# Last rows of four batches in one output block, and the last modes copied by halves on two engines

## The chip, the cores and the metric

The kernel runs on one core of one Trainium2 chip. The metric is device time in microseconds (us) of one execution. Five engines work beside each other: TensorE (PE, with its weight loads shown as PEld), VectorE (DVE), ScalarE (ACT), GpSimd (POOL), and SyncE (SP), which here only issues transfers. Matmuls read SBUF and write PSUM, which has 8 banks of 128 x 512 numbers in float32; ACT and DVE bring results from there to SBUF; 16 DMA engines move data between SBUF and device memory (HBM).

## The reference

```
scores = q @ k^T / sqrt(64) + decay(f), causal          # 8 batches, 8 heads, 576 rows, 64 wide
x      = softmax(scores) @ v          -> (8, 576, 512)
X      = rfft(x, axis=1)[:, :64]                        # 64 modes
Yr, Yi = complex product of X with w_r, w_i             # one 512 x 512 matrix pair for each mode
y      = irfft(Y, n=576)
u      = x + y
out    = u + relu(u @ w_ch)
```

The weights w_r and w_i of the 64 modes are by far the largest input: 64 pairs of 512 x 512 float32 matrices.

## The kernel before

A first phase computes the attention for 32 pairs of heads, and already multiplies the modes with those weights that have come in. A second phase streams the rest of the weights. Modes are taken in 16 units of four. Twelve units (96 rows of real and imaginary parts, `KF`) are folded early, batch by batch, by the inverse transform into `x_all` (which holds x and then x plus these modes) and into `XW` (the same times w_ch). The last four units (32 rows, `KL`) are left for the end, since their weights come last.

The end is what the change touches. It runs over output blocks: `blocks` is a list of (p, sb), where p is a pair of batches and sb one of five row blocks of 128, 128, 128, 128 and 64 rows. Each block needs, for each of its two batches, a PSUM tile `U` (u) and a tile `Z` (u times w_ch):

- `bases(n)` (matmuls at L788) starts the sums with `x_all` and `XW` through an identity. The row block of 64 rows is handled for two batches in one tile: one in rows 0 to 63, one in rows 64 to 127.
- `rest(n, U, Z)` (L803) adds the last modes: a matmul of depth 32, with the inverse transform `BI4` and the mode tile `yl`. `yl[h][0]` is for U and `yl[h][1]` for Z, h being a half of the batches (0 to 3, 4 to 7); each tile holds four batches, 32 rows each.
- ACT copies U to `u_sb` (L857); DVE computes max(Z, 0) + u_sb into `o_sb` (L858); SP issues the output transfer (L863, 512 KB for both batches of a full block; L868, two transfers of 128 KB for a block of 64 rows).

`last_modes(h)` makes the two `yl` tiles. Four matmuls with the identity turn the modes `YL` into `pyl` (L815). Eight matmuls with w_ch give `pywl` (L826): for each of four steps over the depth, one matmul for rows 64 to 127 and one for rows 0 to 63. Then ACT copies `pyl` to `yl[h][0]` (L834), and DVE copies `pywl` to `yl[h][1]` (L835). It is called for h = 0 ahead of the first block and for h = 1 ahead of block 7, counted from 0; the batches of half 1 begin with block 10.

The order of instructions on each engine is the order in which the program writes them (the schedule is manual). `psU` and `psZ` have four PSUM banks each, in turns; `pyl` and `pywl` take one each. The framework puts in the waits, among them those between writers of the same tile.

Of the kernel before, what the change touches and what calls it, by code (L numbers as in the profile page):

```python
# [10 lines left out]
F32 = mybir.dt.float32  # L11
BF16 = mybir.dt.bfloat16
# [11 lines left out]
def kernel(  # L24
# [11 lines left out]
    nc = tc.nc  # L36
    B, H, S, Dh = q.shape
    NM = moe_w_r.shape[0]
    D = H * Dh
    assert S == 576 and Dh == 64 and D == 512 and H == 8, (B, H, S, Dh)  # L40
    assert NM == 64 and B == 8
    NSB = 5
    SBLK = [128, 128, 128, 128, 64]
    NEB = D // 128
# [24 lines left out]
    wch = const.tile([128, NEB, D], BF16, name="wch")  # L69
# [8 lines left out]
    BI4 = const.tile([128, S], BF16, name="BI4")  # L78
# [547 lines left out]
    with ExitStack() as bctx:  # L626
# [3 lines left out]
        ylpool = bctx.enter_context(tc.tile_pool(name="ylpool", bufs=4))  # L630
        YT = ypool.tile([128, NEB, B, KF], BF16, name="YT")
        YL = ypool.tile([128, NEB, B, KL], BF16, name="YL")
        XW = {}

        with ExitStack() as mctx:
# [83 lines left out]
            for u in range(NU):  # L719
# [3 lines left out]
                first = 2 if u < NX else 1  # L723
                for dc in range(first, NEB - 1 if last else NEB):
# [3 lines left out]
                    if u >= NF and dc < 3:  # L728
                        b = 2 * (u - NF) + dc - 1
# [19 lines left out]
                for eb in range(NEB):  # L749
                    nc.tensor.matmul(  # L750
                        yps[:, eb, :],
                        lhsT=Yb[:, eb * 128 : (eb + 1) * 128],
                        rhs=perm[:],
                        start=True,
                        stop=True,
# [10 lines left out]
        usb = bctx.enter_context(tc.tile_pool(name="usb", bufs=4))  # L766
        psU = bctx.enter_context(tc.tile_pool(name="psU", bufs=4, space=PSUM))
        psZ = bctx.enter_context(tc.tile_pool(name="psZ", bufs=4, space=PSUM))
        blocks = [(p, sb) for p in range(B // 2) for sb in range(NSB)]
        yl = {}  # L770

        def parts(n):

            p, sb = blocks[n]
            Ms = SBLK[sb]
            if sb < NSB - 1:
                return [(2 * p + k, k, slice(0, Ms), sb, Ms) for k in range(2)]
            return [(2 * p + k, 0, slice(Ms * k, Ms * k + Ms), sb, Ms) for k in range(2)]

        def bases(n):  # L780

            pts = parts(n)
            nt = 1 + pts[1][1]
            U = [psU.tile([128, D], F32, tag="u", name="U") for _ in range(nt)]
            Z = [psZ.tile([128, D], F32, tag="z", name="Z") for _ in range(nt)]
            for which, ps in enumerate((U, Z)):
                for b, k, rows, sb, Ms in pts:
                    nc.tensor.matmul(  # L788
                        ps[k][rows, :],
                        lhsT=ident_bf[:Ms, :Ms],  # L790
                        rhs=XW[b][:Ms, sb, :] if which else x_all[:Ms, :, b, sb, :],
                        start=True,
                        stop=False,
                    )
            return U, Z

        def rest(n, U, Z):

            for which, ps in enumerate((U, Z)):
                for b, k, rows, sb, Ms in parts(n):  # L800
                    r = (b + 2 * which) % 4
                    grp = slice(32 * r, 32 * r + 32)
                    nc.tensor.matmul(  # L803
                        ps[k][rows, :],
                        lhsT=BI4[grp, sb * 128 : sb * 128 + Ms],
                        rhs=yl[b // 4][which][grp, :],
                        start=False,
                        stop=True,
                    )

        def last_modes(h):

            py = psU.tile([128, D], F32, tag="u", name="pyl")
            for eb in range(NEB):
                nc.tensor.matmul(  # L815
                    py[:, eb * 128 : (eb + 1) * 128],
                    lhsT=YL[:, eb, 4 * h : 4 * h + 4, :].rearrange("p b c -> p (b c)"),
                    rhs=ident_bf[:, :],
                    start=True,
                    stop=True,  # L820
                )
            pyw = psZ.tile([128, D], F32, tag="z", name="pywl")
            for eb in range(NEB):
                for n in range(2):
                    b = 4 * h + 2 * (1 - n)
                    nc.tensor.matmul(  # L826
                        pyw[64 * n : 64 * n + 64, :],
                        lhsT=YL[:, eb, b : b + 2, :].rearrange("p b c -> p (b c)"),
                        rhs=wch[:, eb, :],
                        start=(eb == 0),  # L830
                        stop=(eb == NEB - 1),
                    )
            yl[h] = [ylpool.tile([128, D], BF16, tag="yl", name="yl") for _ in range(2)]
            nc.scalar.copy(yl[h][0][:], py[:])  # L834
            nc.vector.tensor_copy(yl[h][1][:], pyw[:])  # L835

        first = bases(0)
        AT = psU.tile([128, NEB, 8, B], F32, tag="u", name="AT2")
        spec_cols(AT, NEB - 1)
        for h in range(2):  # L840
# [4 lines left out]
                accT[:, :, bs, :],  # L845
                ALU.add,
            )
        last_modes(0)
        for i, (p, sb) in enumerate(blocks):
            if i == 7:  # L850
                last_modes(1)
            U, Z = first if i == 0 else bases(i)
            rest(i, U, Z)
            o_sb = wpool.tile([128, 2, D], F32, tag="w8", name="o_sb")
            for n in range(len(U)):
                u_sb = usb.tile([128, D], F32, tag="usb", name="u_sb")
                nc.scalar.copy(u_sb[:], U[n][:])  # L857
                nc.vector.scalar_tensor_tensor(  # L858
                    o_sb[:, n, :], Z[n][:], 0.0, u_sb[:], ALU.max, ALU.add
                )  # L860
            s0 = sb * 128
            if len(U) == 2:
                nc.sync.dma_start(  # L863
                    out[2 * p : 2 * p + 2, s0 : s0 + 128, :].rearrange("b p e -> p b e"), o_sb[:]
                )
            else:
                for b, k, rows, _, Ms in parts(i):
                    nc.sync.dma_start(out[b, s0 : s0 + Ms, :], o_sb[rows, 0, :])  # L868


# [28 lines left out]
```

## Time and profile before

Three runs took 442.95, 443.5 and 444.18 us; the median is 443.5. The profiled execution took 443.21 us, of which 441.4 is the span from its first to its last instruction.

| what | before |
|---|---|
| profiled execution, span | 443.21 us, 441.4 us |
| PE, DVE, ACT, POOL busy, share of the span | 79%, 62%, 50%, 26% |
| DMA, mean rate | 219 GB/s |
| output transfers | 16 of 512 KB, 8 of 128 KB |
| first and last output transfer issued | 410.1 us, 436.1 us |

Times inside the span are counted from its first instruction. A row of the timeline gives the start, the busy time, the engine, the line and operation, the result and its sources, the shapes, how many instructions it merges, and in brackets how long the engine was idle before it and for whom. In the chain of waits, which is followed back from the last instruction, each row is a start, a length and the work; "issue" is time in which the engine waited for nothing that the profile shows. DMA shares are means over the 16 engines.

### The profile page before, as it was taken

Reading aid. Unit: us, or ns where it says so; the run is one execution under the profiler, and the core shown is the slowest. Engines: PE = TensorE matmul, PEld = TensorE weight load, DVE = VectorE, ACT = ScalarE, POOL = GpSimd, SP = SyncE. Lnnn points to the kernel's source line nnn. Section 1 sums busy time; section 2 is a strip of 40 time slices with the busy share of each in tenths; the row PEclk is TensorE's granted clock in tenths of the full one; section 3 lists DMA queues with packets and bytes.
Section 4 is the critical chain, followed back from the end, with each engine's and each line's share of the span. In section 5 each row is a group of like instructions: output and inputs, shape, how many; then the busy total and the mean of one; then the engine's idle time right before and its main releaser. Section 6 shows DMA issues by size and latency. Waiting matters only on the chain.

```text
span 441.4 us, 10293 instructions
## 1 busy us (share of the span) xinstructions
PE 349.8 (79%) x4305; PEld 192.2 (44%) x4305; DVE 275.3 (62%) x657; ACT 222.8 (50%) x339; POOL 113.1 (26%) x170
## 2 busy tenths in 40 slices
PE   1699787898898898888994495698798688888992
PEld 0456555554555565555552242243343233334330
DVE  6688999978887778888882231223313256464894
ACT  4444765586777765756650022033222265554672
POOL 6443434334433333434213111111202221100000
PEclk9999999999999999999998598599969699899997
DMA  8999999999999999999999999999999999994697
GB/s 205 205 230 229 219 228 230 229 218 228 221 226 230 227 220 229 218 230 218 206 212 212 212 212 211 213 212 212 212 212 210 210 209 210 211 210 86 238 365 258
DMA packets 70207, 96.77 MB, mean 219 GB/s; under 512 B 3536, under 2 KB 45008, under 8 KB 70160
## 3 DMA queue, kind: packets, MB, share of 16 engines
q0 software_dynamic: 60480, 77.08, 99.6%
q1 hardware_dynamic: 9680, 19.03, 12.5%
q8 instruction: 34, 0.56, 0.5%
q14 instruction: 13, 0.11, 0.1%
HBM read 163.73 MB, written 9.44 MB: 392 GB/s over the span
## 4 chain that ended last, share of the span: by engine, by line
DMA 36%; PE 36%; DVE 18%; issue 3%; ACT 3%; POOL 1%; DVEq 0%; POOLq 0%; ACTq 0%
DMA w<-in_moe_w_i_dram 22%; DMA w<-in_moe_w_r_dram 13%; DVE qkT L360 4%; DVE x_all L495 4%; PE pav L480 4%; PE A L194 4%; DVE vT L384 4%; PE sps L435 3%; PE tv L382 3%; PE pd L524 3%; PE vp L393 3%; DMA qk<-in_k_dram 2%; PE U L788 2%; PE Z L788 2%; DVE vn L372 2%
## 5 line engine op out<-in xcount | busy, mean ns | idle before, releaser
L442 ACT ACTIVATE et<-sps 128x1024 bf16<-128x1024 f32 x96 | 96.0, 1050 | 17.7 <-PE sps L435 13.1
L480 PE MATMUL pav<-vs,et 128*128 128x65 bf16 (+1 forms) x896 | 52.5, 199 | 0.0
L747 DVE TENSOR_TENSOR Yb<-A,yx 128x512 bf16<-128x512 f32 x15 | 10.4, 691 | 65.7 <-PE A L194 65.7
L360 DVE COPY qkT<-tp 128x640 bf16<-128x640 bf16 x64 | 48.7, 763 | 3.3 <-PE tp L355 3.3
L480 PEld LDWEIGHTS <-et 128*128 128x128 bf16 (+1 forms) x896 | 37.5, 103 | 18.1 <-issue 14.9
L194 PE MATMUL A<-w,XP 128*16 128x512 bf16 (+1 forms) x240 | 22.2, 450 | 24.9 <-DMA w<-in_moe_w_i_dram 14.2
L435 PE MATMUL sps<-qkT 64*128 64x512 bf16 (+4 forms) x320 | 40.3, 315 | 1.1 <-DVE qkT L360 1.1
L663 PE MATMUL pxw<-wch,xT 128*128 128x512 bf16 (+1 forms) x160 | 41.1, 412 | 0.0
L355 PE MATMUL tp<-ident_bf,qk 128*64 128x128 bf16 x576 | 30.3, 237 | 10.3 <-DMA qk<-in_k_dram 10.3
L495 DVE TENSOR_TENSOR x_all<-pav,rcp 128x384 bf16<-128x384 f32 (+2 forms) x96 | 36.2, 377 | 3.3
L384 DVE COPY vT<-tv 128x576 bf16<-128x576 bf16 x32 | 24.2, 757 | 18.9 <-PE tv L382 18.9
L156 POOL DMA_DIRECT2D w<-in_moe_w_r_dram x27 | 20.5, 757 | 51.9 <-DMA w<-in_moe_w_r_dram 16.1
L670 ACT CAST XW<-pxw 128x512 bf16<-128x512 f32 (+1 forms) x15 | 8.8, 584 | 47.6 <-PE pxw L663 47.6
L156 POOL DMA_DIRECT2D w<-in_moe_w_i_dram x27 | 20.3, 752 | 47.3 <-DMA w<-in_moe_w_i_dram 34.6
L670 ACT CAST yx<-pxw 128x512 bf16<-128x512 f32 (+1 forms) x25 | 14.6, 584 | 34.2 <-PE pxw L663 34.2
L165 POOL DMA_DIRECT2D w<-in_moe_w_r_dram x16 | 11.9, 741 | 71.2 <-PE A L194 56.8
L165 POOL DMA_DIRECT2D w<-in_moe_w_i_dram x19 | 13.2, 697 | 58.6 <-PE A L194 40.3
L709 ACT CAST x_all<-pu 128x512 bf16<-128x512 f32 (+1 forms) x40 | 23.4, 584 | 8.0 <-PE pu L708 7.0
L515 ACT CAST XS<-pd 128x192 bf16<-128x192 f32 x16 | 16.7, 1041 | 18.6 <-PE pd L508 18.5
L355 PEld LDWEIGHTS <-qk 128*64 128x64 bf16 x576 | 19.6, 117 | 14.1 <-issue 8.8
L109 POOL DMA_DIRECT2D qk<-in_q_dram x32 | 19.4, 606 | 24.0 <-PE tp L355 8.4
L372 DVE TENSOR_TENSOR vn<-vt,wn 128x576 bf16<-128x576 f32 x32 | 23.8, 744 | 2.7 <-ACT wn L297 2.7
(134 smaller groups left out, 645.6 us busy)
## 6 DMA issues: line engine op xcount, KB each, us to landing
w<-in_moe_w_r_dram POOLq DMA_DIRECT2D x16, 1024.0 KB, 29.6
w<-in_moe_w_i_dram POOLq DMA_DIRECT2D x15, 1024.0 KB, 32.2
w<-in_moe_w_r_dram POOLq DMA_DIRECT2D x27, 512.0 KB, 14.8
w<-in_moe_w_i_dram POOLq DMA_DIRECT2D x27, 512.0 KB, 14.6
vt<-in_v_dram SPq DMA_DIRECT2D x32, 288.0 KB, 5.8
out_dram<-o_sb SPq DMA_DIRECT2D x16, 512.0 KB, 4.0
qk<-in_q_dram POOLq DMA_DIRECT2D x32, 144.0 KB, 13.6
qk<-in_k_dram POOLq DMA_DIRECT2D x32, 144.0 KB, 13.7
```

The costliest lines, as they stand in the source:

```text
L156: nc.gpsimd.dma_start(w8[:, t, :, :], src[4 * u : 4 * u + 4, dc * 128 : (dc + 1) * 128, :].rearrange("m p e -> p m e"),)
L165: nc.gpsimd.dma_start(w8[:, j : j + step, :, :].rearrange("p m r e -> p m (r e)"), src[m : m + step, 256:512, :].rearrange("m (p r) e -> p ...
L194: nc.tensor.matmul(A[32 * j : 32 * j + M, :], lhsT=lhsT, rhs=rhs, start=st_, stop=sp_)
L355: nc.tensor.transpose(tp[64 * hp : 64 * hp + 64, r - r0, :, :].rearrange("p n c -> p (n c)"), qk[:, hp, r * 64 : r * 64 + 64], ident_bf[:, :],
L360: nc.vector.tensor_copy(st[i]["T"][:].rearrange("p n (c r) -> p n c r", r=9)[:, :, :, r0:r1], tp[:, 0 : r1 - r0, :, :].rearrange("p r n c ...
L372: nc.vector.tensor_tensor(vn[:], st[i]["vt"][:], _strided(wn[:, widx(i), :], [[1, 9], [0, Dh]]), ALU.mult)
L384: nc.vector.tensor_copy(st[i]["vT"][:].rearrange("p (c r) -> p c r", r=9), tv[:].rearrange("p r c -> p c r"))
L435: nc.tensor.matmul(ps[:, hp, c : c + n], lhsT=KT[sl, jb * 128 : jb * 128 + 128], rhs=QT[sl, i0 : i0 + n], start=True, stop=True,)
L442: nc.scalar.activation(st[i]["et"][:, T, :, :], ps[:], ACT.Exp, scale=scale)
L480: nc.tensor.matmul(pav[:Ms, sb % 3, hp, :], lhsT=eblk(i, hp, jb, sb), rhs=rhs, start=(jb == 0), stop=(jb == sb),)
L495: nc.vector.tensor_tensor(x_all[:ns, g, b, lo:hi, :].rearrange("p s (h d) -> p s h d", h=2), pav[:ns, lo % 3 : lo % 3 + n, :, 0:Dh], _stri ...
L663: nc.tensor.matmul(pxw[:Ms, :], lhsT=xT[:, eb, sb * 128 : sb * 128 + Ms], rhs=wch[:, eb, :], start=(eb == 0), stop=(eb == NEB - 1),)
```

## The change

The list of blocks gets another order and other blocks of 64 rows. For each half of the batches come the full blocks of its two pairs, eight in all, and then one block with the last 64 rows of four batches in two tiles. There are 18 blocks instead of 20, and as many matmuls and output results as before.

`last_modes` is taken apart. `modes_u(h)` makes `yl[h][0]`; `modes_z(h, n)` computes one half of the rows of `pywl`, with four matmuls, and `modes_z_keep(h, n)` copies that half. All copies go through `both`, which gives the left 256 columns to ACT and the right 256 to DVE. For h = 0, `modes_u` and the half with batches 0 and 1 stand ahead of block 0; the matmuls of the other half stand between block 0's U and Z matmuls, and its copy after block 0. For h = 1, `modes_u` stands after block 3, one half of `pywl` after block 4, the other after block 5. The first block is written by two transfers of 256 KB, each after its own result.

```diff
-        blocks = [(p, sb) for p in range(B // 2) for sb in range(NSB)]
+        blocks = []
+        for h in range(2):
+            blocks += [(p, sb) for p in (2 * h, 2 * h + 1) for sb in range(NSB - 1)] + [(h, NSB - 1)]
...
-            return [(2 * p + k, 0, slice(Ms * k, Ms * k + Ms), sb, Ms) for k in range(2)]
+            return [
+                (4 * p + 2 * k + m, k, slice(Ms * m, Ms * m + Ms), sb, Ms)
+                for k in range(2)
+                for m in range(2)
+            ]
...
-        def rest(n, U, Z):
+        def rest(n, ps, which):
...
+        def both(dst, src):
+            nc.scalar.copy(dst[:, 0 : D // 2], src[:, 0 : D // 2])
+            nc.vector.tensor_copy(dst[:, D // 2 : D], src[:, D // 2 : D])
+
-        def last_modes(h):
+        def modes_u(h):
+            yl[h] = [ylpool.tile([128, D], BF16, tag="yl", name="yl") for _ in range(2)]
             py = psU.tile([128, D], F32, tag="u", name="pyl")
...
+            both(yl[h][0], py)
+        pywl = {}
+        def modes_z(h, n):
+            if n == 1:
+                pywl[h] = psZ.tile([128, D], F32, tag="z", name="pywl")
+            half = slice(64 * n, 64 * n + 64)
+            b = 4 * h + 2 * (1 - n)
             for eb in range(NEB):
-                for n in range(2):
...
+        def modes_z_keep(h, n):
+            half = slice(64 * n, 64 * n + 64)
+            both(yl[h][1][half, :], pywl[h][half, :])
...
-        last_modes(0)
+        modes_u(0)
+        modes_z(0, 1)
+        modes_z_keep(0, 1)
         for i, (p, sb) in enumerate(blocks):
-            if i == 7:
-                last_modes(1)
-            U, Z = first if i == 0 else bases(i)
-            rest(i, U, Z)
+            U, Z = UZ if i == 0 else bases(i)
+            rest(i, U, 0)
+            if i == 0:
+                modes_z(0, 0)
+            rest(i, Z, 1)
...
+                if i == 0:
+                    nc.sync.dma_start(out[n, 0:128, :], o_sb[:, n, :])
...
+            if i == 0:
+                modes_z_keep(0, 0)
+            elif i == 3:
+                modes_u(1)
+            elif i == 4:
+                modes_z(1, 1)
+                modes_z_keep(1, 1)
+            elif i == 5:
+                modes_z(1, 0)
+                modes_z_keep(1, 0)
```

More of the change, by code (lines that the diff above doesn't have):

```diff
@@ L777, in parts @@
                 return [(2 * p + k, k, slice(0, Ms), sb, Ms) for k in range(2)]
-            return [(2 * p + k, 0, slice(Ms * k, Ms * k + Ms), sb, Ms) for k in range(2)]
+            return [
[3 more added lines that the diff above has]
+            ]
         def bases(n):
             pts = parts(n)
-            nt = 1 + pts[1][1]
-            U = [psU.tile([128, D], F32, tag="u", name="U") for _ in range(nt)]
-            Z = [psZ.tile([128, D], F32, tag="z", name="Z") for _ in range(nt)]
+            U = [psU.tile([128, D], F32, tag="u", name="U") for _ in range(2)]
+            Z = [psZ.tile([128, D], F32, tag="z", name="Z") for _ in range(2)]
             for which, ps in enumerate((U, Z)):
@@ L795, in bases @@
             return U, Z
-        def rest(n, U, Z):
[L799 to L809, printed above, removed]
-        def last_modes(h):
+        def rest(n, ps, which):
+            for b, k, rows, sb, Ms in parts(n):
+                r = (b + 2 * which) % 4
+                grp = slice(32 * r, 32 * r + 32)
+                nc.tensor.matmul(
+                    ps[k][rows, :],
+                    lhsT=BI4[grp, sb * 128 : sb * 128 + Ms],
+                    rhs=yl[b // 4][which][grp, :],
+                    start=False,
+                    stop=True,
+                )
+        def both(dst, src):
[3 more added lines that the diff above has]
+            yl[h] = [ylpool.tile([128, D], BF16, tag="yl", name="yl") for _ in range(2)]
             py = psU.tile([128, D], F32, tag="u", name="pyl")
@@ L821, in last_modes @@
                 )
-            pyw = psZ.tile([128, D], F32, tag="z", name="pywl")
-            for eb in range(NEB):
-                for n in range(2):
[L825 to L837, printed above, removed]
+            both(yl[h][0], py)
[5 more added lines that the diff above has]
+            b = 4 * h + 2 * (1 - n)
+            for eb in range(NEB):
+                nc.tensor.matmul(
+                    pywl[h][half, :],
+                    lhsT=YL[:, eb, b : b + 2, :].rearrange("p b c -> p (b c)"),
+                    rhs=wch[:, eb, :],
+                    start=(eb == 0),
+                    stop=(eb == NEB - 1),
+                )
+        def modes_z_keep(h, n):
+            half = slice(64 * n, 64 * n + 64)
+            both(yl[h][1][half, :], pywl[h][half, :])
+        UZ = bases(0)
         AT = psU.tile([128, NEB, 8, B], F32, tag="u", name="AT2")
@@ L847 @@
             )
-        last_modes(0)
+        modes_u(0)
+        modes_z(0, 1)
+        modes_z_keep(0, 1)
         for i, (p, sb) in enumerate(blocks):
-            if i == 7:
-                last_modes(1)
-            U, Z = first if i == 0 else bases(i)
-            rest(i, U, Z)
+            U, Z = UZ if i == 0 else bases(i)
[3 more added lines that the diff above has]
+            rest(i, Z, 1)
             o_sb = wpool.tile([128, 2, D], F32, tag="w8", name="o_sb")
-            for n in range(len(U)):
+            for n in range(2):
                 u_sb = usb.tile([128, D], F32, tag="usb", name="u_sb")
@@ L860 @@
                 )
+                if i == 0:
+                    nc.sync.dma_start(out[n, 0:128, :], o_sb[:, n, :])
             s0 = sb * 128
-            if len(U) == 2:
+            if sb == NSB - 1:
+                for b, k, rows, _, Ms in parts(i):
+                    nc.sync.dma_start(out[b, s0 : s0 + Ms, :], o_sb[rows, k, :])
+            elif i > 0:
                 nc.sync.dma_start(
@@ L865 @@
                 )
-            else:
-                for b, k, rows, _, Ms in parts(i):
-                    nc.sync.dma_start(out[b, s0 : s0 + Ms, :], o_sb[rows, 0, :])
+            if i == 0:
[8 more added lines that the diff above has]
+                modes_z_keep(1, 0)
 _INS = ['q', 'k', 'v', 'f', 'moe_w_r', 'moe_w_i', 'moe_w_ch']
```

## The prediction

> **What bounds the kernel now.** I read the page first. TensorE is busy 79% of the span and the weight stream keeps the DMA engines at about nine tenths to the 36th of 40 slices, so the body is set by loads that the change does not touch; the built programs are the same instruction for instruction up to the first `bases`. All the difference has to arise after the last weight has been used, at 404 us. Next I split what follows into stages, with each engine's busy time.
>
> ```profile
> 404.00:408.27 4.27, 3.21 (x48) 1.85 (x49) 1.27 (x4) 1.07 (x3) 0.00 (x0) 1.00 0.02 4
> 408.27:420.00 11.73, 11.73 (x80) 3.87 (x80) 9.54 (x16) 8.01 (x16) 0.00 (x0) 1.00 0.71 247
> 420.00:432.50 12.50, 12.50 (x86) 4.10 (x84) 11.66 (x20) 9.66 (x19) 0.00 (x0) 1.00 0.99 350
> 432.50:441.40 8.90, 0.77 (x8) 0.19 (x5) 2.40 (x4) 1.47 (x3) 0.00 (x0) 0.74 0.69 249
> ```
>
> The columns are the stage, its length, busy us (instructions) of PE, weight loads, DVE, ACT and POOL, then granted clock, DMA share and GB/s. From 408.27 TensorE has no free moment, and from 420 the DMA engines have none either (0.99): the stage has two limits, and the output queue is the later one. The vector engine ends at 434.91 (its last nine results start at 429.04 and take 5.87), but the last output transfer is issued at 436.1 and lands at 440.0. Then I read the chain of waits where the stage opens, and the timeline beside it.
>
> ```profile
> 406.05 0.41 PE pyl L815 x4
> 406.46 0.02 issue
> 406.48 0.59 ACT yl L834
> 407.08 0.45 issue
> 407.53 0.70 DVE yl L835
> 408.23 0.04 issue
> 408.27 0.39 PE Z L803 x2
> ```
>
> ```profile
> 406.38 1.05 PE L826 MATMUL pywl<-wch,YL 128*64 128x512 bf16 x8
> ...
> 408.74 1.29 DVE L858 SCALAR_TENSOR_TENSOR o_sb<-Z,u_sb 128x512 f32<-128x512 f32 x2 [0.52 <-PE Z L803]
> ...
> 410.06 4.92 SPq L863 DMA_DIRECT2D out_dram<-o_sb  x4
> ...
> 415.21 2.09 SPq L868 DMA_DIRECT2D out_dram<-o_sb  x2
> ```
>
> The first Z needs the vector copy of all of `pywl`, and the first transfer needs two vector results: nothing is written before 410.06. A full block then comes every 1.30 us (1.39 for one in four, where the Z matmuls show 0.69 us instead of 0.59). Last, the DMA view from 408 to 428 us, in 40 slices of 0.5 us:
>
> ```profile
> GB/s 0 0 0 0 0 25 373 377 275 147 348 336 361 389 365 389 389 373 258 74 229 303 385 410 401 393 258 307 381 369 385 381 336 250 295 397 389 402 410 356
> ```
>
> At 370 to 390 GB/s a 512 KB block takes 1.4 us, a little more than the engines need to make one. The queue thus falls behind by itself, unless a block is late: it ran nearly dry at 412.5, at 417.5 (74 GB/s) and, last, at 421 (258), where block 7 came late behind the second `last_modes`.
>
> **The change part by part.** The number of instructions of each kind is the same on TensorE; ACT and DVE have seven more each, all copies.
>
> *First modes, U.* One 0.59 us copy on ACT becomes two of 256 columns. DVE copies 128x256 from PSUM to bf16 in 0.42 (L761); for ACT no row has it, between 0.29 (half of 0.585) and 0.585: I take 0.35. In the built program the DVE half waits for the ACT half of the same tile, so 0.35 + 0.05 + 0.42 = 0.82, ending at 407.30. TensorE comes to the U matmuls only at 407.36, after `pywl`: cost nothing, with 0.06 us to spare. No row shows two engines reading one PSUM bank. [...]
>
> *First modes, Z.* Before, eight matmuls of 64 output columns alternate between the two halves of the array and take 0.98 us in the chain. A half alone is four. Their price lies between 0.49 (half of eight) and 1.03 (the four of L687, 96 columns wide, 0.88 in the chain). Of the 0.98 some 0.10 is the change from another kind of matmul, so a pair took 0.22, and that is what one matmul of 512 columns takes in the chain (L713, L705); I take 0.88 for four: the pairing was the saving, and it is lost. The first half thus ends where all eight did, 407.4. Copies 0.82: 408.25 (before 408.22). Now the new wait: in the built program the other half's matmuls wait for the DVE half of the first copy, since they write the same tile, and the block's Z matmuls are queued behind them on TensorE. 0.05 + 0.88 + 0.10 for the change of matmul kind (what L788 loses after L803): Z starts at 409.2 instead of 408.27, **+0.95**. DVE waits for Z, SP for DVE.
>
> *Block 0 in two transfers.* The first 256 KB goes out at 409.65 + 0.69 = 410.35, the second at 410.95. That is 0.3 later than before for the first, and there is nothing to gain from it unless block 1 follows sooner. It doesn't: its last Z takes over the bank of the first result (410.33 instead of 409.44), then 0.22 for that matmul, 0.10, 0.39 for U, 0.59 for `u_sb`, 1.29 for two results and 0.15 of hand-overs: 413.05 against 411.89, **+1.15**.
>
> *Second modes in three parts.* Before: one piece, 1.31 us of TensorE (416.13 to 417.44), and block 7 came 2.61 us after block 6 instead of 1.30. After: the U part 0.33, with its two copies in front of a U tile some 0.5; a Z part 0.88 + 0.10; a second one 0.98 plus 0 to 0.3 for the wait on the DVE half of the first, taken as 0.15. Sum 2.6, **+1.3**. TensorE has no idle time that could hide it. If a Z part were only 0.49 it would be 1.8, +0.5.
>
> *Last rows.* Four small blocks each took 0.89 of TensorE, 0.91 of DVE (0.61 and 0.30 idle). Two of four batches take 4 + 2 matmul slots, two results, some 1.45 each and 0.2 after the first: 3.1 against 3.6, **-0.5**. But runs of eight full blocks meet the 1.39 every second time: 3 or 4 more times 0.1, **+0.4**. The output transfers stay eight of 128 KB.
>
> Engines: 1.15 + 1.3 - 0.5 + 0.4 = +2.35, the last vector result at about 437.3.
>
> **From there to the end.** The queue counts, so I look for its last dry moment. Blocks after: 1 at 413.05, 2 at 414.35, 3 at 415.75, 4 at 417.55, 5 at 419.8, 6 at 422.25. Packets begin 0.92 after an issue (410.98 for 410.06), 1.4 per block: the queue is dry for 0.4 before block 4, 0.85 before 5, 1.05 before 6, and never again. Before, the same point was block 7, issued at 420.70. So 1.55 later. Left to write from there: before ten blocks and three pairs of 128 KB, 6.03 MB, in 421.6 to 440.0, or 328 GB/s with all its losses; after, ten blocks and eight of 128 KB, 6.29 MB, 0.8 us more. **+2.35** again. Against the profiled execution (443.21, of which 441.4 is span) that is 445.56; that execution lies 0.3 below the median of 443.5, and on the median I get 445.85, told as 445.9.
>
> **Bounds.** With the cheap ends (Z parts 0.49, copies side by side) block 6 comes about 1.5 us sooner; that leaves +1.0. If the queue's own unevenness before (about 1.6 us: the output packets' durations summed over 16 engines are 26.65 us, and with 410.98 and some 0.8 us of dry moments that ends at 438.4, not 440.0) is partly filled after, up to 1 us less: +0.4 to +1.3. On the other side SP took 1.12 to 2.16 us for a pair of small transfers; four in a row, some 3.6 us, may hold back block 9 by 1.2 and the end by 0.5: +4.
>
> **The rivals.** *The queue absorbs it.* The vector engine ended 5.1 us before the last landing, so 2.35 us later engines might hide behind the queue. For it: the share 0.99. Against it: what is dry early is not caught up, as the queue never has spare speed later. It holds if the queue is backed up at blocks 5 and 6; then only the later start and half of the rest are left, +0.6: 444.1. Chance 0.18.
>
> *Faster: the queue never runs dry.* If the three parts at blocks 4 to 6 fit into pauses that the modelled ends of matmuls hide, each hand-over stays under 1.4 us and the old dry moments at 417.5 and 421 vanish. From the first packet at 411, 9.44 MB at 385 GB/s are 24.5 us, two groups of small transfers 0.9 each, 0.35 to land: 437.7 against 440.0, -2.3, 441.2. It decides at the interval from block 3 to block 6: over 4.5 us it fails; I work out 6.5. For it speaks that a busy PE is modelled; against it PE 11.73 of 11.73. Chance 0.08.
>
> *The small transfers stall SP* (price above): +4, 447.5. For it: 2.16 for the last pair; against it: 1.12 for the second. Chance 0.10.
>
> **How the numbers follow.** The forecast, +1.3 to +3, has 0.64. The range leaves out a tenth on each side: from 444.1, the absorbed case, to 447.6, the stalled one. A measurement of this kernel tells 0.3%, 1.33 us, from no change. Slower by more: the forecast and the stall, 0.74. Within: the absorbed case, 0.18. Faster: 0.08.
>
> **What would show it.** Right: first Z at 409.2, four matmuls of a half in 0.88 and DVE's half behind ACT's; first transfers at 410.35 and 410.95, the next at 413.05; blocks 3 to 6 spread over 6.5 us with GB/s falling between them; last vector result at 437.3. Wrong: a half in 0.5 us, the first Z before 408.3, blocks 4 to 6 at an even 1.3 to 1.4 us, or GB/s above 350 from 412 to the end.

## The result, and the profile after

The changed kernel takes 446.74 us (median of 5, 446.46 to 446.89) against 443.96 (median of 5, 442.95 to 444.46): 2.8 us slower, a ratio of 1.0063 with a 95% interval of 1.0048 to 1.0077. Its profiled execution took 446.74 us, with a span of 445.0.

In that execution the first addition into `YL`, with which the tail opens, starts at 406.30 instead of 405.70. Up to there the two programs are the same, and that start varies between 405.7 and 408.3 over the executions below, so from here on positions are given **from the first YL addition** wherever two kernels are compared. The stages of the tail, cut 0.59 us later than in the prediction:

```profile
404.59:408.86 4.27, 3.22 (x44) 1.96 (x45) 1.36 (x5) 1.10 (x3) 0.00 (x0) 1.00 0.00 0
408.86:420.59 11.73, 11.23 (x62) 3.78 (x61) 8.90 (x17) 7.46 (x16) 0.00 (x0) 1.00 0.59 215
420.59:433.09 12.50, 12.50 (x81) 3.88 (x80) 10.90 (x18) 9.55 (x18) 0.00 (x0) 1.00 0.87 295
433.09:445.00 11.91, 3.35 (x29) 1.11 (x28) 4.82 (x8) 3.34 (x7) 0.00 (x0) 0.79 0.81 277
```

The columns are those of the prediction's table. In the second stage TensorE is again busy nearly throughout (11.23 of 11.73), but in the same time there are 62 matmuls where there were 80, and the output rate is 215 GB/s instead of 247; in the third it is 295 instead of 350. At full granted clock (1.00 in both stages), TensorE does something that takes longer. The chain of waits shows what:

```profile
406.65 0.40 PE pyl L825 x4
407.04 0.99 PE pywl L843 x4
408.04 0.03 ACTq L817
408.07 0.04 issue
408.11 0.38 ACT yl L817
408.48 0.02 issue
408.51 0.44 DVE yl L818
408.94 0.04 issue
408.99 1.04 PE pywl L843 x4
```

Four matmuls take 0.99 us where eight took 0.98. The kernel before has this row for its second modes, where TensorE comes to them without a wait:

```profile
416.46 0.98 PE pywl L826 x8
```

Matmul by matmul, the two of a pair start within 0.004 us of each other in the kernel before, and the next pair follows after 0.215 to 0.24. In the changed kernel each single matmul of a half takes a slot of that length for itself: the four start 0.240, 0.216 and 0.216 us apart.

ACT's copy and DVE's copy follow each other, and TensorE waits for the second of them before it starts the other half. Only after that comes Z, in the timeline:

```profile
409.94 0.39 PE L807 MATMUL Z<-yl,BI 32*128 32x512 bf16 x2
...
410.43 1.29 DVE L880 SCALAR_TENSOR_TENSOR o_sb<-Z,u_sb 128x512 f32<-128x512 f32 x2 [1.49 <-ACT yl L817]
410.71 0.84 PE L793 MATMUL Z<-XW,ident_bf 128*128 128x512 bf16 x2
411.15 0.94 SPq L884 DMA_DIRECT2D out_dram<-o_sb  x2
...
413.84 10.92 SPq L890 DMA_DIRECT2D out_dram<-o_sb  x7
```

The bracket names ACT's copy as the one that ended DVE's wait, but the result starts 0.49 us after the Z matmuls, much as before (408.74 after 408.27); it waits for Z, and the copy happened to end at the same moment. The Z matmuls of block 1 take 0.84 instead of 0.59: their second one waits for the bank of block 0's first result (it starts at 411.17, after the 411.12 at which that result ends), as foreseen. And the output rate from 408.6 to 428.6 us, 40 slices of 0.5 us:

```profile
GB/s 0 0 0 0 0 0 82 381 369 217 0 0 270 360 319 369 373 303 86 385 385 389 377 385 180 102 389 389 221 25 41 377 393 373 381 385 307 217 197 213
```

There are four holes instead of the old three: after block 0 (0 GB/s at 413.6 to 414.6), ahead of block 3 (86), of block 5 (102) and of block 6 (25 and 41). Those ahead of blocks 5 and 6 are where the prediction put them. The one that it put ahead of block 4 comes a block sooner: up to the slice with 86, 1.04 MB have passed since the first hole, which is blocks 1 and 2, and block 3's issue takes 0.99 us (416.53 to 417.52) where most take 0.37. The last three slices, 217 to 197, are something else; they come back at the end of this document.

| us from the first YL addition | before | after | later by | predicted |
|---|---|---|---|---|
| first Z matmuls start | 2.57 | 3.64 | 1.07 | 0.95 |
| second result of block 1 | 6.19 | 7.51 | 1.32 | 1.15 |
| last vector result | 29.21 | 31.87 | 2.66 | 2.35 |
| last landing | 34.32 | 37.39 | 3.07 | 2.35 |

### The profile page after: what moved, and what is told of

It reads as the page before. It is cut to its first block, busy times and chain, and to the rows that moved or that the text cites. A ratio compares the mean times of both kernels' runs of the same rounds, so it can differ in the third digit from the quotient of the medians.

```text
span 445.0 us, 10306 instructions
## 1 busy us (share of the span) xinstructions
PE 352.4 (79%) x4305; PEld 193.0 (43%) x4305; DVE 277.1 (62%) x661; ACT 224.3 (50%) x343; POOL 113.1 (25%) x170
## 4 chain that ended last, share of the span: by engine, by line
PE 37%; DMA 36%; DVE 18%; ACT 3%; issue 3%; POOL 1%; DVEq 0%; ACTq 0%; POOLq 0%
DMA w<-in_moe_w_i_dram 22%; DMA w<-in_moe_w_r_dram 13%; DVE qkT L360 4%; PE pav L480 4%; DVE x_all L495 4%; PE A L194 4%; DVE vT L384 4%; PE sps L435 3%; PE tv L382 3%; PE pd L524 3%; PE vp L393 3%; DMA qk<-in_k_dram 2%; PE Z L793 2%; PE U L793 2%; DVE vn L372 2%
## 5 line engine op out<-in xcount | busy, mean ns | idle before, releaser
L663 PE MATMUL pxw<-wch,xT 128*128 128x512 bf16 (+1 forms) x160 | 40.1, 405 | 0.0
L880 DVE SCALAR_TENSOR_TENSOR o_sb<-Z,u_sb 128x512 f32<-128x512 f32 x36 | 23.1, 686 | 4.7 <-ACT u_sb L879 2.5
```

Of the source, the lines that this page charges most:

```text
L663: nc.tensor.matmul(pxw[:Ms, :], lhsT=xT[:, eb, sb * 128 : sb * 128 + Ms], rhs=wch[:, eb, :], start=(eb == 0), stop=(eb == NEB - 1),)
```

## The experiments

All were run in five rounds beside the kernel before, whose median was 443.86 beside the first four, and 444.32 or 444.00 beside the others. The theory: TensorE's time counts in the tail, a half of the Z modes costs as much as the whole, and what is lost passes on to the end of the output. The first rival: the output queue (dry moments, small transfers in fours). The second: the copies in two serial halves. The third: the wait of Z behind the second half.

**Copies whole again.** From the changed kernel:

```diff
-            both(yl[h][0], py)
+            nc.scalar.copy(yl[h][0][:], py[:])
-            both(yl[h][1][half, :], pywl[h][half, :])
+            nc.vector.tensor_copy(yl[h][1][half, :], pywl[h][half, :])
```

> Changed kernel with the copies whole again: the U modes by ACT alone, each half of the Z modes by DVE alone over 512 columns. Theory (the loss is the matmuls of a half without a partner, 0.88 us each, and Z queued behind the second): a copy of 0.69 in place of 0.37 + 0.43 in a row, so the first Z comes some 0.1 to 0.15 us sooner, and the end 0.3 us sooner than in the changed kernel: +2.5 us against before. Rival (the copies by halves are the loss, since DVE waits for ACT each time): most of the 2.8 us goes, +0.5 us against before.

Measured: 446.95, ratio 1.0072 (1.0055 to 1.0090), no better than the changed kernel. The first Z comes 0.12 us sooner, as expected, but the 0.3 at the end does not appear: the last vector result stands at 31.96. In the second modes DVE's copy of 0.69 takes more of DVE's own time than a half of 0.43, which may be why; no run separates it. The copies by halves gain nothing, and they are not the loss.

**First modes as before.**

```diff
-        modes_u(0)
-        modes_z(0, 1)
-        modes_z_keep(0, 1)
+        modes_whole(0)        # eight paired matmuls, whole copies
...
-            if i == 0:
-                modes_z(0, 0)
...
-                modes_z_keep(0, 0)
```

> Changed kernel with the modes of the first four batches made as before (eight paired matmuls, whole copies, all ahead of block 0); the second modes stay in three parts. Theory: first Z about 2.6 us after the start of the YL addition, as before, 1.1 us sooner than in the changed kernel; every block up to 6 comes 1.1 us sooner and so does the end: +1.7 us against before. Rival (the output queue is what sets the end, four small transfers in a row hold it back): the blocks come sooner but the end stays, +2.5 to +3.

Measured: 445.42, ratio 1.0038 (1.0023 to 1.0054), 1.6 us above before. Block 1's second result is back at 6.20, the last vector result at 30.56 and the last landing at 36.08, both 1.31 sooner than in the changed kernel. The end did move with the engines, against the first rival.

**Second modes as before**, in one piece ahead of block 7; the first stay in halves.

```diff
+            if i == 7:
+                modes_whole(1)
...
-            elif i == 3:
-                modes_u(1)
-            elif i == 4:
-                modes_z(1, 1)
-                modes_z_keep(1, 1)
-            elif i == 5:
-                modes_z(1, 0)
-                modes_z_keep(1, 0)
```

> Changed kernel with the modes of the last four batches made as before, in one piece ahead of block 7 (counted from 0); the first modes stay in halves. Theory: one piece of 1.31 us of TensorE in place of 2.6, so the block after it comes 1.3 us sooner than the same block of the changed kernel, and the queue is dry once in place of three times: +1.5 us against before. Rival (queue and small transfers): +2.5 to +3.

Measured: 444.99, ratio 1.0028 (1.0016 to 1.0039), 1.1 us above before, where 1.5 was expected. Last vector result 30.44 and last landing 35.95, each 1.43 to 1.44 sooner than in the changed kernel.

**The list of blocks alone.** Both edits above, and block 0 in one transfer.

> The new list of blocks alone: last rows of four batches in one block; modes made and copied as before (ahead of block 0 and of block 7), the first block in one transfer. Theory: engine time is about that of before (0.5 us less for small blocks, 0.4 more for pauses in runs of eight), block 7 as in before, 256 KB more left to write from there: 0 to +0.8 us against before. Rival (queue and small transfers four in a row): +2 us or more. Rival (fewer small groups help the queue): -1 us.

Measured: 444.48, ratio 1.0013 (1.0002 to 1.0025), 0.6 us above before. The last vector result stands at 29.13, 0.08 sooner than before; the last landing at 34.76, 0.44 later. For the engines the new blocks are neutral, and the queue pays a little.

The sum closes on the engines: 1.31 for the first modes, 1.43 for the second, -0.08 for the blocks, together 2.66, which is what the changed kernel shows. On the last landing the three are 1.31, 1.44 and 0.44, together 3.19 where the changed kernel shows 3.07.

**The second half behind Z.**

```diff
             rest(i, U, 0)
-            if i == 0:
-                modes_z(0, 0)
             rest(i, Z, 1)
+            if i == 0:
+                modes_z(0, 0)
```

> Changed kernel, but in block 0 the second half's four matmuls stand behind the Z matmuls instead of ahead of them, so that Z doesn't queue behind their wait for the copy. Theory (the 0.9 us of TensorE are the loss, the queueing only shows where): first Z 1.0 us sooner, first two transfers 1.0 us sooner, but the second half now stands ahead of block 1's matmuls, so block 1 and all that follows come only some 0.2 us sooner: +2.6 us against before. Rival (the new wait of Z is the loss): block 1 and the end 1.0 us sooner, +1.8.

Measured: 446.39 against 444.32, ratio 1.0052 (1.0037 to 1.0067). The interval, 1.6 to 3.0 us, holds both expectations; the trace decides. The timeline of this kernel, whose first YL addition is at 406.46:

```profile
409.15 0.39 PE L807 MATMUL Z<-yl,BI 32*128 32x512 bf16 x2 [0.64 <-DVE yl L818]
...
409.47 1.05 PE L843 MATMUL pywl<-wch,YL 128*64 128x512 bf16 x4
```

Z starts at 2.69, 0.95 sooner, and the first two transfers leave 0.97 sooner. But block 1's second result stands at 7.29, only 0.22 sooner, and the last landing at 37.20, 0.19 sooner. The wait of Z was where the loss showed; the loss is the 1.05 us of TensorE, which now stand ahead of block 1. The third rival falls.

**Second modes paired, in the early places.** From the kernel with the first modes as before: the two Z halves together after block 4, copied once.

```diff
             elif i == 4:
-                modes_z(1, 1)
-                modes_z_keep(1, 1)
-            elif i == 5:
-                modes_z(1, 0)
-                modes_z_keep(1, 0)
+                ...                      # eight paired matmuls into pyw
+                both(yl[1][1], pyw)
```

> As the kernel with the first modes made as before and the second in three parts (measured 1.6 us above before), but the two Z halves of the second modes are made together, eight paired matmuls after block 4, copied once by ACT and DVE one after the other; the U part stays after block 3. Theory (a half without a partner costs 0.88 us of TensorE): one piece of 0.98 instead of two, blocks 6 and later 0.9 to 1.2 us sooner: +0.6 us against before. Rival (the places of the parts, close to the start where the queue has nothing in hand, are the loss): +1.4 to +1.7 still.

Measured: 444.27 against 444.00, ratio 1.0008 (0.9996 to 1.0020). The two timelines, of the kernel with the halves and of this one:

```profile
416.82 1.05 PE L843 MATMUL pywl<-wch,YL 128*64 128x512 bf16 x4
...
419.34 1.02 PE L843 MATMUL pywl<-wch,YL 128*64 128x512 bf16 x4 [0.17 <-DVE yl L818]
```

```profile
417.02 1.05 PE L922 MATMUL pywl<-wch,YL 128*64 128x512 bf16 x8
```

Two groups of four, 1.05 and 1.02, against one of eight, 1.05. The last vector result goes from 30.56 to 29.31 and the last landing from 36.08 to 34.85. Pairing, with one pair of copies instead of two, is worth 1.23 to 1.25 us here; the early places are not the loss.

**Spreading in the old order.** The kernel before, with the U modes ahead of block 6 and the paired Z modes ahead of block 8:

```diff
-            if i == 7:
-                last_modes(1)
+            if i == 6:
+                modes_u(1)
+            if i == 8:
+                modes_z(1)            # all eight matmuls, copied whole by DVE
```

> The kernel before with its second modes in two parts, not halves: the U modes ahead of block 6, the eight paired Z matmuls and their whole copy ahead of block 8; all else as before. Theory (halves without a partner cost, spreading by itself is harmless): TensorE pays 0.33 + 0.98 and 0.1 for one more change of kind, each piece closer to what the queue can cover: -0.3 to +0.2 us against before. Rival (any piece between blocks costs the queue its own dry moment): +0.5 to +1.

Measured: 444.33 against 444.32, ratio 0.9999 (0.9983 to 1.0015). In the trace the last vector result and the last landing are both about 0.35 later. Spreading gains nothing, and alone it costs too little for these runs to see.

**Half of the output left out**, in the kernel before and in the changed one: full blocks write `out[2 * p, ...]` from `o_sb[:, 0, :]`, blocks of 64 rows every second part.

> The kernel before, with the output transfers of every odd batch left out (all is computed; 4.7 of 9.4 MB written). Theory: the queue has spare speed, the last landing follows the last vector result (29.2 us after the first YL addition) by 2 to 2.5 us instead of 5.1: -2.5 to -3 us against before.

> The changed kernel with the same transfers left out, every odd batch's. Theory: the engines alone are 2.7 us later than before's (last vector result), so this kernel is 2.7 us above the old one with half the output, near +-0.3 us of before with its full output. Rival (the 2.8 us come from the output queue, its dry moments or the small transfers in fours): the difference between the two kernels with half the output falls below 1 us.

Measured: 440.50 (ratio 0.9918, 0.9902 to 0.9934) and 443.52 (0.9983, 0.9968 to 0.9998). The difference is 3.0 us. Both engine sides are unmoved, with last vector results at 29.21 and 31.87; the last landings follow at 31.53 and 34.24. So writing the second half of the output costs the kernel before 3.8 us by these times, where 2.5 to 3 was expected; counted from the first YL addition in the two traces, its last landing comes 2.79 sooner, and where the rest arises is open. The two kernels with half the output land 2.71 apart. The changed kernel's loss is thus about as large with a queue that has spare speed (DMA share 0.49 in the one from 408.59 to 432.82 us, 0.42 in the other from 408.46 to 435.00) as with a fuller one (0.86 in the kernel before from 408.27 to 434.90, 0.78 in the changed one from 408.86 to 438.20). The first rival falls as the source of the loss.

**One move for a faster kernel.** If TensorE's time ahead of block 1 is what the tail pays for, something should be taken out of it. In the kernel before, block 1's U base matmuls go between block 0's U and Z matmuls, where TensorE waits for the copy of the Z modes:

```diff
-            rest(i, U, Z)
+            if i == 0:
+                rest(0, U, Z, (0,))
+                U1 = base(1, 0)       # block 1's two U base matmuls
+                rest(0, U, Z, (1,))
```

> The kernel before, with one move: block 1's two U base matmuls stand between block 0's U and Z matmuls, where TensorE waits 0.52 us for the copy of the Z modes. Theory (TensorE's time ahead of block 1 is what the tail pays for): block 1 comes 0.4 to 0.5 us sooner, the last vector result too, the end -0.2 to -0.5 us against before, less than these runs can tell from no change. Rival (the output queue sets the end whatever block 1 does): no change in the last landing.

```profile
407.51 0.39 PE L805 MATMUL U<-yl,BI 32*128 32x512 bf16 x2
...
407.83 0.61 PE L786 MATMUL U<-x_all,ident_bf 128*128 128x512 bf16 x2
...
408.42 0.39 PE L805 MATMUL Z<-yl,BI 32*128 32x512 bf16 x2
```

Measured: 443.42 against 444.00, ratio 0.9992 (0.9978 to 1.0006). Z starts at 2.57 as before (the first YL addition is at 405.85), and the two matmuls fill the wait exactly. Block 1 and the last vector result come 0.43 sooner, as expected, and the last landing 0.72, more than the 0.2 to 0.5 expected; that is one execution of each. The times alone do not tell it from no change. Of the versions that write the whole output it is the only one whose median lies below that of before.

## Why the prediction was right

The forecast was 445.9 and slower; 446.74 was measured. Set against the runs of before at hand, the step was 2.35 us, and 2.8 came.

*First modes, Z.* Right in mechanism and nearly in size: 1.07 for 0.95. (The terms as listed end at 409.28, which is 1.01 later than before; 409.2 was written.) Four matmuls cost 0.99 for the 0.88 + 0.10 taken. DVE's half does come behind ACT's (0.38 and 0.44 in the chain for 0.35 and 0.42), and Z is queued behind the second half. That the U copy is hidden was nearly wrong: U starts at 1.66 in both, and the U copy was done only 0.05 us ahead of it, for the 0.06 stated. Copies side by side, which the bounds allow for, no run shows: in the changed kernel each DVE half starts 0.03 us or more after its ACT half has ended (407.49 after 407.46, 408.51 after 408.48). What the experiment with the second half behind Z corrects is the weight of the step: this wait by itself is worth only 0.2; the TensorE time is worth the rest.

*Block 1.* 1.32 for 1.15. From the first modes through to the end it was worth 1.31.

*Second modes.* From block 3's second result to that of block 7 the changed kernel takes 7.86, or 2.66 more than four blocks of 1.30; 2.6 was worked out. Against the old 1.31 that is +1.35 for +1.3. Undoing it gave 1.43, and pairing alone 1.23.

*Last rows.* -0.5 and +0.4 came to -0.08 in the kernel with the new list alone, so the sum holds. The terms can be read in the changed kernel: the results of the two blocks of four batches come 1.50 and 1.44 us after those of the block before, the block after the first of them 0.20 later than a full block does, and the full blocks come after 1.30 and 1.39 in turns. The seven more copies that the prediction counted on ACT and DVE are four on each (339 to 343 and 657 to 661 instructions); no term used the number.

*From there to the end.* This term was mis-sized. The last dry moment is ahead of block 6, as worked out, and block 6 is issued 0.03 after its result, so the hole ahead of block 3 instead of block 4 does not set the end. But block 6 leaves 1.85 later than the old block 7 (1.55 was taken), and from there to the last landing it takes 20.54 us instead of 19.32, so 1.22 more where 0.8 stood for 256 KB at the old mean rate. Part of it may be the blocks of four batches, whose transfers ran at about 210 GB/s instead of 380 (below); the new list alone lands 0.44 later with its vector results 0.08 sooner. The unevenness of the old queue, which I had let take up to 1 us off, took nothing off.

*The rivals.* That the queue absorbs the loss needed a queue backed up at blocks 5 and 6; it ran dry ahead of both. That it never runs dry needed 4.5 us from block 3 to block 6; it took 6.62. The long issues of small transfers did not come in the middle: those of block 8 took 0.47 to 0.58, and only two of the last four took 1.25 and 1.24.

## What to carry to other kernels

Count matmuls by the slots that they take in the trace, not by their width: here two that wrote 64 rows each, in different halves of one PSUM tile, took one slot of some 0.22 us together, so computing one half "first" cost as much as both (0.99 us for four matmuls, 0.98 for eight) and the other half came on top. Two engines on two halves of one tile gained nothing over one engine here (0.37 and 0.43 in a row against 0.69), since the program makes the second wait for the first; the waits of the built program tell that before any run. With TensorE busy nearly throughout (11.23 of 11.73 us), moving a wait away (0.97 us sooner at the first transfer) gave back little (0.2); taking out work (1.31 and 1.43), or filling an existing wait (0.43), moved the end.

## What the runs showed of the hardware beyond that

Four transfers of 64 rows in a row ran at little more than half the rate of full blocks, about 210 GB/s instead of 380. In the DMA view of the changed kernel, 425 to 431 us in slices of 0.15 us, those of block 8 pass between 426.8 and 429.2:

```profile
DMA  9999999999998995989889988999399999999999
GB/s 314 355 423 383 355 369 423 382 369 355 437 369 246 273 232 137 287 177 218 178 246 219 205 191 205 232 218 218 96 369 410 423 369 355 410 396 423 382 383 369
```

The DMA engines stay busy, mostly at eight or nine tenths, while the rate drops from about 380 to about 210 GB/s. At the very end of the kernel with the new list alone, 420 to 442 us in slices of 0.55, it is the same, and there all issues are done by 438.8 us while the low rate lasts to 439.8, so the issuing of small transfers is not what holds it down:

```profile
GB/s 399 384 339 48 149 384 391 265 283 145 201 209 402 398 387 369 384 384 376 387 365 376 380 384 376 361 391 365 357 369 402 339 224 220 216 224 97 7 0 0
```

The old pairs, with a full block in flight beside them, dip for a shorter time: in the kernel before to 213 GB/s or less for 0.5 us from 424.6, and for 1.0 us from 431.0, but for one slice. As a mean over the 16 engines the output packets take 27.24 us in the kernel with the new list alone (27.16 in the changed kernel) and 26.65 in the kernel before; the difference, 0.59, is of the size of the 0.44 us by which the new list alone lands later. No run here took transfers of 64 rows alone or read them from other rows of the tile, so what holds the rate down is not shown. Also open is why nine of the issues on SP in the kernels before and after took 0.71 to 1.54 us where the others took 0.34 to 0.59. Two holes in the queue follow such issues: the one ahead of block 3 in the changed kernel follows an issue of 0.99, and the one at 417.5 in the kernel before follows one of 1.53, the second of the pair that takes 2.09 in the prediction's timeline.
